# Attention and a two-layer product on one core: one more ff pair by seven half-size products, and another order and store for the last tile

## The chip, the cores and the metric

The kernel runs on one core of a Trainium2 chip. The metric is the device time of one execution in microseconds (us). TensorE (PE) multiplies matrices, VectorE (DVE), ScalarE (ACT) and GpSimd (POOL) work element by element, and SyncE (SP) issues most of the transfers (DMAs). In the profile, PEld is the loading of weights into TensorE, and a "q" behind an engine's name (SPq) is its instruction queue.

## The reference, cut to what matters

```python
def _attn_ref(q, k, v):                      # B, H, S, D = 4, 8, 768, 64
    k_sum = k.reshape(B, H, nb, block, D).max(axis=3)      # block = 32
    v_sum = v.reshape(B, H, nb, block, D).mean(axis=3)
    scores_l = scale * np.matmul(q, k.transpose(0, 1, 3, 2))   # kept within 16 of the diagonal
    scores_s = scale * np.einsum('bhsd,bhnd->bhsn', q, k_sum) + np.log(block)
    ...                                      # softmax over both, then times [v, v_sum]

def _moe_ref(x, w_in, w_out):                # x: 3072 x 512, w_in: 512 x 2048, w_out: 2048 x 512
    h = x @ w_in
    g = h * (1.0 / (1.0 + np.exp(-1.702 * h)))
    return (g @ w_out).astype(np.float32)
```

The attention's output, with the heads put side by side, is the `x` of the second function.

## The kernel before, in words

The work goes batch by batch (4 batches of S = 768 rows). For each batch the attention gives x, turned so that the model dimension lies on the partitions: four tiles `xTT[half][g]`, with the left half of the rows (384, called l) and the right half (r). The last two of them come by DMA transposes from SP. Then the two products follow: "ff", which is x times w_in and the gelu into `gTb`, and "out", which is g times w_out. While one batch is in its products, the attention of the next is put between them. The last batch has no next one, and its products stand alone; the change is there (from `mid.close()` to the end of the kernel function).

Every engine's instructions run in the order in which the code issues them (the class `_Ordered` holds them to it), so the order of the work is the order of the Python statements.

*ff in the last batch.* The 16 ff tiles of 128 columns of w_in are taken as 8 pairs (j and j + 8). A pair's result is four blocks of 128 x 384: two tiles by two halves. `plain(nt, half, tag)` works one block out directly: 4 matmuls of 384 columns and a gelu on ACT. The other way (`ff_product`, `ff_copy`, `ff_gelu`) is a fast 2 x 2 block product with seven products instead of eight: the model dimension is split in two as well, sums of weights (`wsi`) and sums of x (`xs`, by `x_sums` on DVE) are made beforehand, and each of the products 1 to 7 is 2 matmuls of 384 columns. They add up in four PSUM banks, called A, B, C and E; DVE makes a copy from A to C ("a") and the sums from A and "s" to B and E ("b" and "c"), ACT copies E to SBUF ("s"), and at the end four gelus read C, B, E and A. Product 7 adds to A after "b" has read it.

The table `steps` says in which slot of a pair each of these steps is issued, and pair after pair follows 7 slots later, so that the steps of three pairs interleave. `PLAIN` is the number of pairs that are worked out directly; before it is 2, so pairs 0 and 1 (eight blocks of 4 matmuls) are plain and 2 to 7 go by seven products. Seven of the eight plain blocks stand ahead of the first product, the eighth in slot 1 between products 1 and 5. The sums of x stand after the fourth plain block.

*out in the last batch.* The same scheme again: for each of three pairs of row tiles (t, of 128 rows on the left and on the right) `product` makes seven products of 8 matmuls of 256 columns. They read g or sums of g (`gs`, four kinds) and w_out or its sums (`ws`). The sums of g of the plain pairs are made on POOL, all four kinds; of the other pairs POOL makes kinds 0 and 1 (the last pair's are made on DVE), and two wide instructions on DVE make kinds 2 and 3 for all of them at once. Product 1 of each t comes early, between the last steps of ff. The others run in the order 5, 6, 2, 7, 3, 4. ACT copies the result of product 6 ("s2") from the bank to which product 7 then adds, and that of 5 ("s5"); DVE adds kept values to those of 2, 7 and 3 on the way into the output tiles (`give`), and ACT copies that of 4. The output tiles o1 (left rows) and o2 (right rows) are stored from SP (`store`), 128 x 512 floats at once; only in the last t is o2 stored in two halves.

Of the kernel before, what the change touches and what calls it, by code (L numbers as in the profile page):

```python
# [35 lines left out]
def kernel(  # L36
# [10 lines left out]
    B, H, S, D = q.shape  # L47
# [4 lines left out]
    d_model, d_ff = moe_w_in.shape  # L52
# [7 lines left out]
    HALF = S // 2  # L60
    TH = NQ // 2
    JH = NJ // 2
# [3 lines left out]
    act = _Ordered(tc, nc.scalar)  # L66
    pool = _Ordered(tc, nc.gpsimd)
    sp = _Ordered(tc, nc.sync)
# [200 lines left out]
    def copy(eng, out, in_):  # L269
        if eng is act:  # L270
            act.activation(out=out, in_=in_, func=ACT.Copy)
        elif eng == "dve_alone":

            dve.tensor_reduce(out=out, in_=in_.unsqueeze(len(in_.shape)), axis=AX.X, op=ALU.max)
        else:
            eng.tensor_copy(out=out, in_=in_)
# [366 lines left out]
    def gelu(half, nt, ph):  # L643
        act.activation(out=gT[half][:, nt, :], in_=ph, func=ACT.Gelu_apprx_sigmoid)
# [3 lines left out]
    def ff_step(ph, half, nt, steps=range(KO)):  # L648
        for n in steps:
            g, i = n // 2, n % 2  # L650
            ko = g + 2 * i if halves[0] else 2 * g + i
            pe.matmul(out=ph, lhsT=w_in_sb[:, ko, nt * 128:(nt + 1) * 128],
                      rhs=xTT[half][g][:, i], start=(n == 0), stop=(n == KO - 1))
# [29 lines left out]
    def g_sums(j, eng=dve, which=(0, 1, 2, 3)):  # L683

        a1, a2 = gTb[:, j], gTb[:, j + NT // 2]
        l, r = slice(0, HALF), slice(HALF, S)
        for w in which:
            a, b_, op = {0: (a1[:, r], a2[:, r], ALU.add), 1: (gs[:, 0, j], a1[:, l], ALU.subtract),
                         2: (a1[:, l], a1[:, r], ALU.subtract), 3: (a2[:, l], gs[:, 1, j], ALU.subtract)}[w]
            eng.tensor_tensor(out=gs[:, w, j], in0=a, in1=b_, op=op)  # L690
# [12 lines left out]
    now = {}  # L703
# [10 lines left out]
    xs = [vflat[:, i * 2 * HALF:(i + 1) * 2 * HALF].rearrange(two, k=2) for i in range(4)]  # L714
# [7 lines left out]
                     2: (a11, a21, ALU.subtract), 3: (a12, wsi[1], ALU.subtract)}[what]  # L722
        dve.tensor_tensor(out=wsi[what], in0=a, in1=b_, op=op)

    def x_sums():

        (l1, l2), (r1, r2) = xTT
        for o, a, b_ in ((0, r1, l1), (1, r2, xs[0]), (2, r2, r1), (3, l2, xs[1])):
            dve.tensor_tensor(out=xs[o], in0=a, in1=b_, op=ALU.subtract)

    plast = {}
# [1 line left out]
    def last_bank(tag, name):  # L733
        return plast[tag in "AB"].tile([128, 512], F32, name=name, tag="last" + tag,
                                       bufs={"A": 3, "E": 2, "B": 1, "C": 2}[tag])
# [39 lines left out]
    def product(b, t, what):  # L775
        n = NT // 2
        l = slice(t * 128, t * 128 + 128)
        r = slice(HALF + t * 128, HALF + t * 128 + 128)
        lo, hi = slice(0, N1), slice(N1, d_model)
        raw_l, raw_r = gTb[:, :, l], gTb[:, :, r]  # L780
        w1, w2 = w_out_sb[:, 0:n], w_out_sb[:, n:]
        lhs, rhs, bank, opens = {
            1: (raw_l[:, 0:n], w1[:, :, lo], "A", True),
            2: (raw_l[:, n:], w2[:, :, lo], "C", True),
            6: (gs[:, 1, :, l], ws[:, 1], "A", False),
            5: (gs[:, 0, :, l], ws[:, 0], "B", True),
            7: (gs[:, 2, :, l], ws[:, 2], "A", False),
            3: (gs[:, 3, :, l], w2[:, :, hi], "B", False),
            4: (raw_r[:, n:], ws[:, 3], "A", False)}[what]
        if opens:  # L790
            now[t, bank] = (last_bank("B" if bank == "A" and t == 2 else {"A": "A", "B": "E", "C": "C"}[bank],
                                      "po" + bank) if b + 1 == B
                            else pmm.tile([128, 512], F32, name="po" + bank, tag="mm"))
        po = now[t, bank][:, 0:N1]
        for i in range(n):
            pe.matmul(out=po, lhsT=lhs[:, i], rhs=rhs[:, i], start=(opens and i == 0),
                      stop=(i == n - 1), skip_group_check=True)

        def keep_it(name):
            if b + 1 == B and name == "s1":  # L800
                t_ = now[t, name] = spare[:, 2 * HALF + t * N1:2 * HALF + (t + 1) * N1]
            else:
                t_ = now[t, name] = snap.tile([128, N1], F32, name=name, tag=name)
            copy(dve if t == 0 and b + 1 < B else act, t_, po)

        def give(o, cols, name):
            if (t, o) not in now:
                now[t, o] = outp.tile([128, d_model], F32, name="osb", tag="osb")
            if name:
                dve.tensor_tensor(out=now[t, o][:, cols], in0=po, in1=now[t, name], op=ALU.add)  # L810
            else:
                act.activation(out=now[t, o][:, cols], in_=po, func=ACT.Copy)

        def store(o, tok, cols=slice(0, d_model)):
            r0 = b * S + tok
            sp.dma_start(out=out[r0:r0 + 128, cols], in_=now[t, o][:, cols])
            if cols.start == 0:
                now.pop((t, o))

        last = b == B - 1 and t == JH - 1  # L820

        if what == 1:
            keep_it("s1")
        elif what == 2:
            give("o1", lo, "s1")
        elif what == 6:
            keep_it("s2")
        elif what == 5:
            keep_it("s5")
        elif what == 7:  # L830
            give("o2", hi, "s5")
            if last:
                store("o2", HALF + t * 128, hi)
        elif what == 3:
            give("o1", hi, "s2")
            store("o1", t * 128)
        else:
            give("o2", lo, None)
            store("o2", HALF + t * 128, lo if last else slice(0, d_model))

    seq = [(0, 1)]
    for t in range(JH):
# [165 lines left out]
    for e in range(2):  # L1008
        r = slice(64 * e, 64 * e + 64)
        dve.tensor_copy(out=w50[r, JH - e:NJ, e, :, 0:D],  # L1010
                        in_=v0n[r, :, JH - e:NJ, 0:D].rearrange("p h j d -> p j h d"))
# [104 lines left out]
    for b in range(1, B - 1):  # L1116
# [32 lines left out]
        i = 0  # L1149
        for t, what in seq:  # L1150
            product(b, t, what)
            if i == 0:
                g_sums(NT // 2 - 1, dve, (2, 3))
            if nxt:
                beside(b + 1, i)
            i += 1
            if nxt and b + 2 < B:
                if i == 1:
                    load_batch(b + 2)
                if i in (16, 18):  # L1160
                    xk(i // 2 - 8, b % 2)
# [2 lines left out]
    for ab in (True, False):  # L1164
        plast[ab] = ctx.enter_context(tc.tile_pool(name=f"plast{ab:d}", bufs=2, space=bass.MemoryType.PSUM))
    b, n = B - 1, NT // 2
    PLAIN = 2

    def plain(nt, half, tag):
        ph = last_bank(tag, "ph")[:, 0:HALF]  # L1170
        ff_step(ph, half, nt)
        gelu(half, nt, ph)

    def ff_do(j, what):
        if isinstance(what, int):
            ff_product(j, what)
        elif what in "asbc":
            ff_copy(j, what)
        elif what == "g":
            g_sums(j, pool, (0, 1))  # L1180
        else:
            ff_gelu(j, what)

    for i, tag in enumerate("CCEEAAA"):
        plain((0, n, 1, n + 1)[i % 4], i // 4, tag)
        if i == 3:
            x_sums()
        if i in (5, 6):
            g_sums(0, pool, (0, 1) if i == 5 else (2, 3))
    steps = {0: [1, "a"], 1: [5, "s"], 9: [7, "c"], 10: [3], 4: [2], 5: [6, "b"], 13: [4],  # L1190
             6: ["C"], 11: ["B"], 12: ["E"], 14: ["A"], 15: ["g"]}
    for slot in range(7 * (n - PLAIN)):
        if slot == 1:
            plain(n + 1, 1, "B")
            g_sums(1, pool, (0, 1, 2, 3))
        for j in range(PLAIN, n):
            for what in steps.get(slot - 7 * (j - PLAIN), ()):
                ff_do(j, what)
    ff_do(n - 2, "A")
    product(b, 0, 1)  # L1200
    ff_do(n - 1, 7)
    ff_do(n - 1, "c")
    ff_do(n - 1, 3)
    ff_do(n - 2, "g")
    ff_do(n - 1, "B")
    ff_do(n - 1, "E")
    product(b, 1, 1)
    g_sums(n - 1, dve, (0, 1))
    ff_do(n - 1, 4)
    ff_do(n - 1, "A")  # L1210
    product(b, 2, 1)
    q_ = slice(PLAIN, n)
    dve.tensor_tensor(out=gs[:, 2, q_], in0=gTb[:, q_, 0:HALF], in1=gTb[:, q_, HALF:S], op=ALU.subtract)
    dve.tensor_tensor(out=gs[:, 3, q_], in0=gTb[:, PLAIN + n:2 * n, 0:HALF], in1=gs[:, 1, q_], op=ALU.subtract)
    for t, what in seq:
        if what != 1:
            product(b, t, what)


# [28 lines left out]
```

## Time and profile before

| | us |
|---|---|
| median of three runs | 206.14 |
| lowest and highest | 206.1, 207.8 |
| the profiled execution | 207.68 |
| its span, from the first to the last instruction | 205.9 |

| engine | busy, us | share of the span | instructions |
|---|---|---|---|
| PE | 199.3 | 97% | 2360 |
| DVE | 140.8 | 68% | 388 |
| ACT | 125.2 | 61% | 239 |
| POOL | 92.1 | 45% | 143 |

The first instruction of the last batch's ff starts at 164.76 us, the last matmul of the kernel ends at 202.35, and the span ends at 205.9.

How to read the lines that follow. In a timeline a row gives the start and the length in us, then the engine, the source line (here always L28, a helper that issues everything), the operation, the tile written, the tiles read, the shape, and how many instructions were put together (x28); a bracket gives the idle time before it and what ended it. Matmuls overlap one another, so in the timeline a group's length reaches 0.16 to 0.17 us into the next one. The chain of work is the sequence of instructions that ended last, followed back from the end; there each row is the time in which that work was what all else waited for. In the rows of DMA issues come the number of transfers, the size of one in KB and the time from issue to landing.

### The profile page before, as it was taken

How to read it: one execution, taken by the hardware profiler on the slowest of the kernel's cores; microseconds unless marked ns; L12 is line 12 of the kernel's file. 1: busy time of each engine (PE TensorE's matmuls, PEld its weight loads, DVE VectorE, ACT ScalarE, POOL GpSimd, SP SyncE). 2: the span in 40 equal slices, each digit the busy share in tenths (PEclk: the TensorE clock that was granted, in tenths of full speed). 3: DMA queues.
4: the chain of work that ended last, by engine and by line, in shares of the span. 5: the costliest groups of instructions: out<-in, count | busy, mean ns of one | idle time of the engine just before them, and what ended most of it. 6: DMA issues, size and time to landing. Idle time of an engine off the chain costs nothing.

```text
span 205.9 us, 5854 instructions
## 1 busy us (share of the span) xinstructions
PE 199.3 (97%) x2360; PEld 138.5 (67%) x2360; DVE 140.8 (68%) x388; ACT 125.2 (61%) x239; POOL 92.1 (45%) x143
## 2 busy tenths in 40 slices
PE   6999999999999999999999999999999999999992
PEld 6668564556754466656888875666888865678882
DVE  6495796594856693899667789896769536758221
ACT  4474975728886726677772446778670577984220
POOL 7974589457999690006970035000000009991000
PEclk9999999999999999999999999999999999999999
DMA  6999999999999999999996979999022640000222
GB/s 174 170 167 205 208 207 207 189 154 243 147 99 162 183 163 171 167 150 159 147 144 87 138 168 127 124 251 172 0 105 73 151 135 3 0 0 3 102 103 102
DMA packets 95850, 28.13 MB, mean 137 GB/s; under 512 B 83648, under 2 KB 92880, under 8 KB 95824
## 3 DMA queue, kind: packets, MB, share of 16 engines
q0 software_dynamic: 69648, 13.24, 80.5%
q1 hardware_dynamic: 26176, 14.52, 33.2%
q8 instruction: 18, 0.29, 0.6%
q14 instruction: 8, 0.07, 0.1%
HBM read 27.26 MB, written 6.29 MB: 163 GB/s over the span
## 4 chain that ended last, share of the span: by engine, by line
PE 89%; DMA 5%; DVE 3%; ACT 1%; issue 0%; SPq 0%; DVEq 0%
PE ph L28 33%; PE poA L28 16%; PE poB L28 8%; PE po L28 8%; PE ps_av L28 4%; PE poC L28 4%; PE phA L28 4%; PE ps_s L28 4%; DMA vw<-vs 3%; DMA gT<-in_k_dram 2%; PE ps_x L28 1%; PE ps_k L28 1%; PE ps_t L28 1%; PE phB L28 1%; PE phC L28 1%; PE ps_q L28 1%
## 5 line engine op out<-in xcount | busy, mean ns | idle before, releaser
L28 PE MATMUL ph<-xT,w_in_sb 128*128 128x384 f16 x416 | 70.2, 326 | 0.1
L28 PEld LDWEIGHTS <-w_in_sb 128*128 128x128 f16 x452 | 43.7, 98 | 27.8 <-issue 0.2
L28 ACT ACTIVATE gT<-ph 128x384 f16<-128x384 f32 x104 | 49.8, 491 | 18.6 <-PE ph L28 18.2
L28 PEld LDWEIGHTS <-gT 128*128 128x128 f16 x312 | 28.8, 98 | 11.0
L28 ACT ACTIVATE a_sb<-ps_s 128x768 bf16<-128x768 f32 (+1 forms) x32 | 25.0, 826 | 12.7 <-PE ps_s L28 12.7
L28 PEld LDWEIGHTS <-gs 128*128 128x128 f16 x288 | 27.7, 98 | 3.4
L28 POOL DMA_DIRECT2D vw<-in_v_dram x36 | 24.6, 705 | 9.4 <-DMA kb<-in_k_dram 4.7
L28 POOL TENSOR_TENSOR gs<-gT 128x384 f16<-128x384 f16 x9 | 8.2, 908 | 43.1 <-ACT gT L28 43.1
L28 PE MATMUL po<-w_out_sb,gT 128*128 128x512 f16 x96 | 23.6, 380 | 0.0
L28 DVE TENSOR_TENSOR a_sb<-a_sb,mk 128x768 bf16<-128x768 bf16 x28 | 14.9, 555 | 6.5 <-ACT a_sb L28 5.9
L28 PE MATMUL poA<-ws,gs 128*128 128x256 f16 x144 | 18.7, 273 | 0.0
L28 DVE TENSOR_TENSOR x<-ps_av,rc 128x384 f16<-128x384 f32 x32 | 17.8, 558 | 1.1
L28 DVE TENSOR_TENSOR gs<-gT 128x384 f16<-128x384 f16 (+1 forms) x34 | 13.3, 393 | 6.9 <-ACT gT L28 6.6
L28 POOL DMA_DIRECT2D qb<-in_q_dram x16 | 15.1, 970 | 3.2 <-DMA v0n<-in_v_dram 1.7
L28 PEld LDWEIGHTS <-kx 64*128 64x128 bf16 (+1 forms) x372 | 9.4, 95 | 6.8 <-issue 4.0
L28 POOL DMA_DIRECT2D kb<-in_k_dram x14 | 13.6, 985 | 0.3 <-issue 0.3
L28 DVE TENSOR_REDUCE ks<-kx 128x24 bf16<-128x768 bf16 x12 | 11.4, 948 | 3.3 <-ACT kx L28 3.0
L28 ACT ACT_TABLE_LOAD x10 | 12.8, 1283 | 1.0 <-PEq L1232 0.8
L28 ACT ACTIVATE osb<-poA 128x256 f32<-128x256 f32 x9 | 3.5, 384 | 15.8 <-PE poA L28 15.8
L28 ACT ACTIVATE s<-poA 128x256 f32<-128x256 f32 x11 | 4.2, 385 | 11.2 <-PE poA L28 11.2
L28 PEld LDWEIGHTS <-a_sb 128*64 128x64 bf16 (+2 forms) x400 | 7.9, 108 | 3.2 <-issue 1.7
L28 PE MATMUL poA<-w_out_sb,gT 128*128 128x256 f16 x72 | 9.4, 273 | 0.0
(117 smaller groups left out, 287.7 us busy)
## 6 DMA issues: line engine op xcount, KB each, us to landing
out_dram<-osb SPq DMA_DIRECT2D x23, 256.0 KB, 3.4
kb<-in_k_dram POOLq DMA_DIRECT2D x14, 192.0 KB, 6.3
qb<-in_q_dram POOLq DMA_DIRECT2D x12, 192.0 KB, 9.4
vw<-in_v_dram POOLq DMA_DIRECT2D x36, 64.0 KB, 5.2
w_out_sb<-in_moe_w_out_dram POOLq DMA_DIRECT2D x4, 512.0 KB, 12.6
w_in_sb<-in_moe_w_in_dram POOLq DMA_DIRECT2D x3, 512.0 KB, 12.5
vw<-vs SPq DMA_DIRECT2D x6, 198.0 KB, 6.7
gT<-in_k_dram SPq DMA_DIRECT2D x2, 384.0 KB, 3.5
```

The lines of the kernel that those rows point to most:

```text
L28: r = f(*a, **kw)
```

## The change

- `PLAIN` goes from 2 to 1: pair 1 too is worked out by seven products, and only pair 0 is plain. Three plain blocks instead of seven stand ahead of the first product, and one still stands in slot 1.
- The sums of x move: three of them stand after the third plain block, the fourth after the plain block of slot 1, which on DVE is behind the copy "a" of the first combined pair.
- POOL makes all four kinds of sums of g for pair 0 alone. The two wide sums on DVE cover seven pairs (2688 columns) instead of six (2304).
- In the last row tile (t = 2) the products run in the order 6, 5, 7, 2, 3, 4. The other two keep theirs.
- In the last row tile o1 too is stored in two halves, each as soon as it is there. The last store of the kernel (the left half of o2) is issued by ACT, which made its last copy, and no longer by SP. That copy is one instruction before and after.

```diff
-    def x_sums():
+    def x_sums(which):
...
-        for o, a, b_ in ((0, r1, l1), (1, r2, xs[0]), (2, r2, r1), (3, l2, xs[1])):
+        for o, a, b_ in [((0, r1, l1), (1, r2, xs[0]), (2, r2, r1), (3, l2, xs[1]))[w] for w in which]:
...
-        def store(o, tok, cols=slice(0, d_model)):
+        last = b == B - 1 and t == JH - 1
+
+        def store(o, tok, cols=slice(0, d_model), queue=sp):
             r0 = b * S + tok
-            sp.dma_start(out=out[r0:r0 + 128, cols], in_=now[t, o][:, cols])
-            if cols.start == 0:
+            queue.dma_start(out=out[r0:r0 + 128, cols], in_=now[t, o][:, cols])
+            if not last:
                 now.pop((t, o))
...
         elif what == 2:
             give("o1", lo, "s1")
+            if last:
+                store("o1", t * 128, lo)
...
         elif what == 3:
             give("o1", hi, "s2")
-            store("o1", t * 128)
+            store("o1", t * 128, hi if last else slice(0, d_model))
+        elif last:
+            give("o2", lo, None)
+            store("o2", HALF + t * 128, lo, act)
         else:
             give("o2", lo, None)
-            store("o2", HALF + t * 128, lo if last else slice(0, d_model))
+            store("o2", HALF + t * 128)
...
-    PLAIN = 2
+    PLAIN = 1
...
-    for i, tag in enumerate("CCEEAAA"):
-        plain((0, n, 1, n + 1)[i % 4], i // 4, tag)
-        if i == 3:
-            x_sums()
-        if i in (5, 6):
-            g_sums(0, pool, (0, 1) if i == 5 else (2, 3))
+    for i, tag in enumerate("CCE"):
+        plain(n * (i % 2), i // 2, tag)
+    x_sums(range(3))
...
         if slot == 1:
-            plain(n + 1, 1, "B")
-            g_sums(1, pool, (0, 1, 2, 3))
+            plain(n, 1, "B")
+            x_sums((3,))
+            g_sums(0, pool, (0, 1, 2, 3))
...
-    for t, what in seq:
-        if what != 1:
+    for t in range(JH):
+        for what in (5, 6, 2, 7, 3, 4) if t + 1 < JH else (6, 5, 7, 2, 3, 4):
             product(b, t, what)
```

More of the change, by code (lines that the diff above doesn't have):

```diff
@@ L812, in give @@
                 act.activation(out=now[t, o][:, cols], in_=po, func=ACT.Copy)
-        def store(o, tok, cols=slice(0, d_model)):
+        last = b == B - 1 and t == JH - 1
+        def store(o, tok, cols=slice(0, d_model), queue=sp):
             r0 = b * S + tok
-            sp.dma_start(out=out[r0:r0 + 128, cols], in_=now[t, o][:, cols])
-            if cols.start == 0:
+            queue.dma_start(out=out[r0:r0 + 128, cols], in_=now[t, o][:, cols])
+            if not last:
                 now.pop((t, o))
-        last = b == B - 1 and t == JH - 1
         if what == 1:
```

## The prediction

> **What bounds the kernel now.** I read the page's total and its chain of work first, then the chain row by row over the last batch, then the timelines of the engines around it, and the DMA issues last. The profiled execution took 207.68 us, of which the span is 205.9 and 1.78 lies around it; the median of the three runs shown is 206.14, so I work out a difference in the span and take it off the median.
>
> ```profile
> span 205.9 us, 5854 instructions
> ...
> PE 89%; DMA 5%; DVE 3%; ACT 1%; issue 0%; SPq 0%; DVEq 0%
> ```
>
> The chain that ends last is matmul after matmul for 89% of the span. In the stage that the change touches, the matmuls in order of time, and then the end of the chain:
>
> ```profile
> 164.76 4.71 PE L28 MATMUL ph<-xT,w_in_sb 128*128 128x384 f16 x28
> 169.31 0.49 PE L28 MATMUL phA<-xT,w_in_sb 128*128 128x384 f16 x2
> ...
> 171.59 0.49 PE L28 MATMUL phE<-vw,kx 128*128 128x384 f16 x2
> 172.14 0.48 PE L28 MATMUL phA<-vw,kx 128*128 128x384 f16 x2
> ```
> ```profile
> 171.52 0.58 DVE phB L28
> ...
> 201.47 0.89 PE poA L28 x8
> 202.35 0.02 issue
> 202.38 0.38 ACT osb L28
> ```
>
> The reader should see a stage that TensorE fills: 28 plain matmuls of 384 columns start between 164.76 and 169.31, 162.5 ns each, back to back. One place breaks the row: the product at 172.14 (7 of the first combined pair) starts 0.55 after the one before it, where two matmuls take 0.33, because it waited for the DVE sum of 171.52: a stall of 0.22. After the last matmul there is one copy (to 202.76), one store and the program's end.
>
> **The change, part by part.**
>
> *Matmuls.* A plain pair of ff tiles takes 2 tiles x 2 halves x 4 matmuls = 16; by seven products it takes 7 x 2 = 14. Pair 1 changes over, so two matmuls go: 2 x 162.5 ns = **-0.33 us**, all of it on the chain, if TensorE still sets the pace. It does in the rounds that exist:
>
> ```profile
> 175.26 0.49 ACT L28 ACTIVATE gT<-phB 128x384 f16<-128x384 f32 x1
> ...
> 182.09 0.49 ACT L28 ACTIVATE gT<-phB 128x384 f16<-128x384 f32 x1
> ```
>
> Three rounds lie between these two rows: 6.83 / 3 = 2.277 us a round, which is 14 x 162.5 ns = 2.275. ACT has five PSUM reads a round (four gelus and the copy "s") and follows without falling behind, so a seventh round adds 2.275 and removes 2.60. DVE gains three adds or copies, ACT one copy; both run beside TensorE at that pace, cost nothing there, and would each cost only what they lag behind 2.275 if that cover went.
>
> *The shorter lead-in.* Before the first product there were 28 plain matmuls, now 12 (pair 0, three of its four tile halves). So everything that prepares that product has 2.60 us less cover. These are the sums of x, and the DMA transposes that they and the third plain tile read:
>
> ```profile
> 164.86 0.56 DVE L28 TENSOR_TENSOR vw<-xT,xT 128x768 f16<-128x768 f16 x1 [0.27 <-DMA xT<-x]
> 166.27 0.56 DVE L28 TENSOR_TENSOR vw<-xT,vw 128x768 f16<-128x768 f16 x1 [0.86 <-DMA xT<-x]
> 166.75 0.55 DVE L28 TENSOR_TENSOR vw<-xT,xT 128x768 f16<-128x768 f16 x1
> 167.22 0.55 DVE L28 TENSOR_TENSOR vw<-xT,vw 128x768 f16<-128x768 f16 x1
> 169.91 0.57 DVE L28 COPY phC<-phA 128x384 f32<-128x384 f32 x1 [2.14 <-PE phA L28]
> ```
>
> The first plain matmul starts at 164.76; product 1 started at 169.31. The third plain tile now starts 8 matmuls in, at 166.06; its third matmul, at 166.39, is the first reader of the last transpose. That transpose had arrived when DVE started at 166.27: cover 0.12. Product 1 falls at 164.76 + 12 x 0.1625 = 166.71. The copy "a" began 0.60 after it (169.91 - 169.31), so now 167.31; DVE is free of the third sum at 167.22, where the fourth began: cover 0.09. The fourth sum is moved behind "a": it starts near 167.79, ends near 168.34, and its reader, product 4, stands 4 us further on. "a" ends at 167.88, product 2 starts at 168.01: the same 0.13 as before. With no wait longer than its cover I cost this part at 0; for each 0.1 us that the transpose is later than 0.12, TensorE loses 0.1. The stall of 0.22 stays, since the plain tile that was put between products 1 and 5 still is.
>
> *Sums for the second stage.* POOL had 18 sums and gets 16 (pairs 0 and 1 were done whole; now only 0), DVE's two wide sums grow from 2304 to 2688 columns:
>
> ```profile
> 185.49 0.68 DVE L28 TENSOR_TENSOR gs<-gT 128x384 f16<-128x384 f16 x1 [0.66 <-ACT gT L28]
> 186.20 0.36 DVE L28 TENSOR_TENSOR gs<-gs,gT 128x384 f16<-128x384 f16 x1
> 186.48 1.35 DVE L28 TENSOR_TENSOR gs<-gT 128x2304 f16<-128x2304 f16 x1
> 187.75 1.35 DVE L28 TENSOR_TENSOR gs<-gT,gs 128x2304 f16<-128x2304 f16 x1
> ```
> ```profile
> 185.04 0.91 POOL L28 TENSOR_TENSOR gs<-gs,gT 128x384 f16<-128x384 f16 x1
> ```
> ```profile
> 189.95 1.04 PE L28 MATMUL poB<-w_out_sb,gs 128*128 128x256 f16 x8
> ```
>
> 1.35 x 2688/2304 = 1.58, so +0.45 us for both. The second ended at 189.10 and ends at 189.10 - 0.33 + 0.45 = 189.22; its reader, product 3, comes at 189.95 - 0.33 = 189.62. Cover 0.40, hence 0; without the cover it would cost the overrun, 0.45 at most. POOL's last sum, which the second wide sum reads, ended at 185.95 and comes earlier.
>
> *The last tile.* Seven products in either order are 56 matmuls, so TensorE's end moves by the 0.33 alone. Product 7 now follows 5 directly behind 6, and adds to the bank that ACT is still copying ("s2"):
>
> ```profile
> 197.81 1.04 PE L28 MATMUL poA<-ws,gs 128*128 128x256 f16 x8
> 198.68 1.04 PE L28 MATMUL poC<-w_out_sb,gT 128*128 128x256 f16 x8
> ```
> ```profile
> 198.88 0.38 ACT L28 ACTIVATE s<-poA 128x256 f32<-128x256 f32 x1 [0.49 <-PE poA L28]
> ```
>
> A product takes 0.87. The copy begins 1.07 after product 6 and ends 1.45 after it; product 7 comes 2 x 0.87 = 1.74 after: cover 0.29, cost 0. The final copy stays one instruction of 0.38, as it was.
>
> *Stores.* Those of the last tile were 128, 256, 128 KB on SP; now three of 128 KB on SP and the last of 128 KB on ACT.
>
> ```profile
> out_dram<-osb SPq DMA_DIRECT2D x2, 128.0 KB, 1.7
> out_dram<-osb SPq DMA_DIRECT2D x1, 256.0 KB, 2.0
> ```
> ```profile
> 202.03 1.09 SPq L28 DMA_DIRECT2D out_dram<-osb  x2
> ```
> ```profile
> L28 SPq DMA_DIRECT2D out_dram<-osb x7: 332/332/333, 191.5 to 202.8; - x7
> ```
>
> The last store was issued about 0.03 after its copy (202.79 to 203.12) and SP was idle by 202.03 + 0.33 = 202.36, so SP held nothing up; it landed 1.7 later, as the first 128 KB store did that had no other behind or ahead of it. Splitting the 256 KB store therefore gains nothing. What is new is a store issued by ACT: no row of before has one. Ends: nothing, less the hand-over of 0.03; or the dearest queue in the trace, POOL's:
>
> ```profile
> L28 POOL DMA_DIRECT2D vw<-in_v_dram x36 | 24.6, 705 | 9.4 <-DMA kb<-in_k_dram 4.7
> ...
> vw<-in_v_dram POOLq DMA_DIRECT2D x36, 64.0 KB, 5.2
> ```
>
> POOL's issue takes 0.71 instead of 0.33 (+0.37), and those loads land after 5.2 instead of 1.7 (+3.5). I take SP's price, 0: its row is of the same transfer, 128 KB of the same tile out to memory with idle DMA engines, while POOL's rows are loads in a crowded stage. Of the end this leaves nothing to win: -0.03 at best, +3.9 at worst.
>
> The Trainium skill has a rule that speaks against expecting anything of this step (DMA: Bandwidth & Descriptors, "Issuing engines are not separate DMA queues"): transfers started by ACT, SP or GpSimd run on the same 16 DMA engines and interleave, so a second issuing engine saves only the time in which the first would have been busy issuing. By that rule the step is worth 0 as well, since SP was idle, and the sum stays where it is; no run here shows a store from ACT yet.
>
> **Sum.** -0.33 + 0 + 0 + 0 + 0: the span goes from 205.9 to 205.57, and the median from 206.14 to **205.8**. About 1% is what a measurement of this kernel can tell from no change; this is 0.16%.
>
> **The rivals.**
>
> *The last transpose comes too late for the shorter lead-in.* The cover is 0.12, and the landing times of these transposes differ:
>
> ```profile
> xT<-x SPq DMA_TRANSPOSE x2, 2.7
> ```
> ```profile
> xT<-x SPq DMA_TRANSPOSE x1, 4.1
> ```
>
> The first row is of the last two, the second of one that shared the engines with a store. For it speaks that nothing else fills these 2.6 us; against it that nothing ahead of 164.8 is changed, so that the transposes should land as they did. If the last took 4.1, it would be 1.4 later, 1.28 beyond the cover: 205.8 + 1.28 = 207.1. From 0.45 on (0.33 + 0.12) the two saved matmuls are given back, which is also the case in which the change does nothing: 206.1.
>
> *The store from ACT is dear* (the other side). It is the last thing on the path, so every bit of it counts whole. If only its issue is as slow as POOL's, 205.8 + 0.37 = 206.2; if it lands like POOL's loads, 205.8 + 3.9 = 209.7. The kernel is slower than before once this store takes 0.33 longer than SP's 1.7, and by over 1% once it takes 2.4 longer. For it: this would be ACT's only transfer, and nothing in the trace shows that queue at work. Against it: the equal work on SP has one price, 332 ns to issue in all seven rows.
>
> *The stall of 0.22 goes too.* Then 205.8 - 0.22 = 205.6. For it: DVE, ACT and POOL are all less loaded in the lead-in. Against it: product 7 waits for a sum that needs product 6, and between them stand only products 1 and 5 of the next pair, as before.
>
> *ACT becomes the bound of the rounds.* Five reads of 0.49 us each are 2.45 in 2.275, and they fit only because they overlap. Were the seventh round to lag by 0.1, the time would be 205.9; the three equal rounds above speak against it.
>
> **How the numbers follow.** I give the forecast 0.74, the late transpose 0.08, the dear store 0.09, the vanished stall 0.05, ACT as the bound 0.04. The likeliest is 205.8 us. The range reaches down to 205.4: the best sum is 206.14 - 0.33 - 0.22 - 0.03 = 205.56, and three runs fix a median no better than to a tenth or two. Upward it reaches to 207.1, the late transpose at its dearest row, which takes in the dear store up to 1.3 more than SP's; what is left out is that store at worse than that and runs like the slowest of the three shown (207.8). A gain of over 1% (below 204.1) has no case: 0.02 for what I overlooked. A loss of over 1% (above 208.2) needs the ACT store near its upper end: 0.05. Within 1%: 0.93.
>
> **What would show it.** In the changed kernel's trace: 12 plain matmuls ahead of the first phA product, starting near 164.8 and 166.7; no wait of the third plain tile for a transpose; one stall of about 0.2 in the first round, and the seven rounds 2.28 apart; the first matmul of the second stage 0.33 earlier; the second wide sum (128x2688, 1.58) done before product 3; ACT's copy of "s2" done before product 7 in the last tile; the last matmul's end near 202.0, the last copy's near 202.4; and the store from ACT issued in about 0.33 and landed in about 1.7. I would be wrong if TensorE's last matmul came at 202.3 or later (a wait took the place of the two matmuls), or if the time from the last copy to the span's end grew beyond the 3.14 of before (205.9 - 202.76).

## The result, and the profile after

| | before | changed |
|---|---|---|
| median of 22 runs each | 206.55 | 205.70 |
| lowest to highest | 205.96 to 208.08 | 205.06 to 207.98 |
| ratio | | 0.9958, 95% interval 0.9941 to 0.9976 |
| ratio on a second occasion (12 and 23 runs) | | 0.9971, 0.9945 to 0.9997 |
| profiled execution; its span | 207.68; 205.9 | 205.72; 203.7 |

The kernel is faster by 0.42% (0.87 us, interval 0.50 to 1.22), and by 0.29% (0.03% to 0.55%) the second time. It stays within 1%, as forecast, and the time lies next to the forecast's 205.8. That nearness is luck in part: the forecast started from the median of three runs, 206.14, which is 0.41 below that of 22, and its gain of 0.33 us is 0.54 short of the 0.87; the two errors nearly cancel. The first interval excludes a gain of 0.33, the second doesn't: the question is where the rest comes from. The change reaches no work ahead of the last batch, yet its first matmul comes 1.46 us earlier in this trace. That says nothing about the change: in the five traces of kernels that are equal up to there (before, e2_tail, e3_act, e5_split and e9_poolless in the table below) it started between 162.8 and 165.7. So the two traces are compared by stretches, not by clock time.

The page of the changed kernel, total and chain of work:

```profile
span 203.7 us, 5850 instructions
...
PE 82%; DMA 9%; DVE 5%; ACT 1%; issue 1%; SPq 0%; ACTq 0%; DVEq 0%
```

TensorE's timeline in the lead-in, and the chain's end:

```profile
163.30 2.11 PE L28 MATMUL ph<-xT,w_in_sb 128*128 128x384 f16 x12
165.25 0.49 PE L28 MATMUL phA<-xT,w_in_sb 128*128 128x384 f16 x2
165.58 0.81 PE L28 MATMUL ph<-xT,w_in_sb 128*128 128x384 f16 x4
...
167.53 0.49 PE L28 MATMUL phE<-vw,kx 128*128 128x384 f16 x2
168.08 0.48 PE L28 MATMUL phA<-vw,kx 128*128 128x384 f16 x2
```
```profile
199.68 0.89 PE poA L28 x8
200.57 0.02 issue
200.59 0.38 ACT osb L28
```

From the first plain matmul to the end of the last matmul it takes 200.57 - 163.30 = 37.27 us by these rows, against 202.35 - 164.76 = 37.59 before; by the trace's nanoseconds 37.251 and 37.576, a difference of 0.325: the two matmuls, to the nanosecond. The lead-in has no new wait, and the old one is there with the old size (167.53 to 168.08 is 0.55 again).

The moved sums and the sums for the second stage, on DVE, with their readers on TensorE and the copy "s2" on ACT:

```profile
164.56 0.56 DVE L28 TENSOR_TENSOR vw<-xT,vw 128x768 f16<-128x768 f16 x1 [0.82 <-DMA xT<-x]
165.04 0.55 DVE L28 TENSOR_TENSOR vw<-xT,xT 128x768 f16<-128x768 f16 x1
165.84 0.57 DVE L28 COPY phC<-phA 128x384 f32<-128x384 f32 x1 [0.26 <-PE phA L28]
...
183.70 0.36 DVE L28 TENSOR_TENSOR gs<-gT 128x384 f16<-128x384 f16 x1 [0.66 <-ACT gT L28]
...
185.84 1.55 DVE L28 TENSOR_TENSOR gs<-gT,gs 128x2688 f16<-128x2688 f16 x1
```
```profile
188.16 1.04 PE L28 MATMUL poB<-w_out_sb,gs 128*128 128x256 f16 x8
...
196.90 1.04 PE L28 MATMUL poA<-ws,gs 128*128 128x256 f16 x8
```
```profile
196.22 0.38 ACT L28 ACTIVATE s<-poA 128x256 f32<-128x256 f32 x1 [0.49 <-PE poA L28]
```

Every cover held. The second wide sum ends at 187.39, 0.77 ahead of product 3 (0.40 forecast: the first small sum takes 0.36 instead of 0.68; before, POOL's last sum ran beside it, and here that had ended at 183.15). "s2" is ready at 196.60, 0.30 ahead of product 7 (0.29 forecast).

Of the end, the last store and its neighbours in the DMA issues, and POOL's part of the instructions with which the program stops, under the names that the trace gives them (semaphores, drains, the clear of a range of semaphores; the same query of before below it):

```profile
out_dram<-osb SPq DMA_DIRECT2D x3, 128.0 KB, 1.7
out_dram<-osb ACTq DMA_DIRECT2D x1, 128.0 KB, 1.7
```
```profile
201.00 0.37 ACTq L28 DMA_DIRECT2D out_dram<-osb  x1
```
```profile
L1247 POOLq EVENT_SEMAPHORE  x4: 17/17/17, 202.9 to 203.6; - x4
...
L1247 POOLq DRAIN  x2: 51/76/102, 203.1 to 203.4; - x2
...
L1247 POOLq EVENT_SEMAPHORE_RANGE_CLEAR  x1: 139/139/139, 203.2 to 203.2; - x1
```
```profile
L1243 POOLq EVENT_SEMAPHORE  x4: 17/17/17, 204.8 to 205.8; - x4
...
L1243 POOLq DRAIN  x2: 102/150/198, 204.9 to 205.5; - x2
...
L1243 POOLq EVENT_SEMAPHORE_RANGE_CLEAR  x1: 139/139/139, 205.1 to 205.1; - x1
```

The reader should look at POOL's last instructions: after the semaphore clear it reaches its last drain in 0.17 us and takes 51 ns for it, where before it took 0.46 and 198 ns. From the clear to the span's end it is 0.45 instead of 0.89, so 0.44 us of the shorter span lies in a place where the kernel computes nothing. With it the time from the last copy's end to the span's end falls from 3.18 to 2.71.

### The profile page after: what moved, and what is told of

The parts are those of the page before. It is cut to its first block, busy times and chain, and to the rows that moved or that the text cites. A ratio compares the mean times of both kernels' runs of the same rounds, so it can differ in the third digit from the quotient of the medians.

```text
span 203.7 us, 5850 instructions
## 1 busy us (share of the span) xinstructions
PE 196.8 (97%) x2358; PEld 136.7 (67%) x2358; DVE 141.6 (70%) x391; ACT 125.4 (62%) x240; POOL 90.3 (44%) x141
## 4 chain that ended last, share of the span: by engine, by line
PE 82%; DMA 9%; DVE 5%; ACT 1%; issue 1%; SPq 0%; ACTq 0%; DVEq 0%
PE ph L28 23%; PE poA L28 16%; PE po L28 11%; PE poB L28 8%; PE ps_av L28 4%; PE phA L28 4%; DMA out_dram<-osb 4%; PE poC L28 4%; PE ps_s L28 3%; DMA qT<-qb 3%; DMA gT<-in_k_dram 2%; DVE ks L28 2%; PE ps_t L28 1%; PE ps_x L28 1%; DVE qT L28 1%; DVE gs L28 1%
## 5 line engine op out<-in xcount | busy, mean ns | idle before, releaser
L28 PE MATMUL ph<-xT,w_in_sb 128*128 128x384 f16 x400 | 67.6, 326 | 0.1
L28 PEld LDWEIGHTS <-w_in_sb 128*128 128x128 f16 x442 | 42.7, 98 | 27.1 <-issue 0.2
L28 ACT ACTIVATE gT<-ph 128x384 f16<-128x384 f32 x100 | 47.9, 492 | 17.9 <-PE ph L28 17.1
L28 POOL TENSOR_TENSOR gs<-gT 128x384 f16<-128x384 f16 x8 | 7.3, 911 | 43.1 <-PE phC L28 42.0
L28 PEld LDWEIGHTS <-kx 64*128 64x128 bf16 (+1 forms) x378 | 10.0, 95 | 7.8 <-issue 4.9
```

The source lines that it names most:

```text
L28: r = f(*a, **kw)
```

## The experiments

Theory 1 was the prediction's: the two matmuls are all, the rest is scatter. Theory 2: the last tile's stores give the rest. Theories 3 and 4 came with the traces of the first four kernels. All kernels in one table; the stretches are from each kernel's one profiled execution, "beyond" is the mean of device time less span over all its runs. POOL's instructions are counted in the traces; the expectations count one more for each kernel.

| kernel | POOL's instructions | first ff matmul to last matmul's end | last copy's end to SP's first drain | clear to span's end | beyond the span | ratio to before (95%) |
|---|---|---|---|---|---|---|
| before | 199 | 37.58 | 1.90 | 0.89 | 1.71 | |
| changed | 195 | 37.25 | 1.86 | 0.45 | 2.01 | 0.9958 (0.9941 to 0.9976) |
| e1_pairs | 195 | 37.25 | 1.90 | 0.45 | 1.99 | 0.9976 (0.9951 to 1.0002) |
| e2_tail | 199 | 37.58 | 1.86 | 0.90 | 1.71 | 1.0000 (0.9971 to 1.0028) |
| e3_act | 199 | 37.58 | 1.94 | 0.89 | 1.72 | 1.0004 (0.9972 to 1.0037) |
| e6_sp | 195 | 37.25 | 1.81 | 0.45 | 2.01 | 0.9973 (0.9940 to 1.0006) |
| e5_split | 199 | 37.58 | 1.81 | 0.89 | 1.68 | one run |
| e9_poolless | 196 | 37.58 | 1.89 | 0.45 | 2.14 | 0.9993 (0.9966 to 1.0021) |
| e10_pad4 | 199 | 37.25 | 1.86 | 0.89 | 1.71 | 0.9998 (0.9972 to 1.0024) |
| e11_pad8 | 203 | 37.25 | 1.86 | 0.45 | 1.74 | one run |
| e11_pad16 | 211 | 37.25 | 1.86 | 0.45 | 1.71 | one run |
| e12_best | 195 | 37.12 | 1.81 | 0.45 | 2.01 | 0.9975 (0.9955 to 0.9995) |
| e14_plain0 | 192 | 37.82; 38.45 from where TensorE was free | 1.86 | 0.45 | 1.88 | 1.0024 (1.0002 to 1.0046) |

### The pairs without the last tile, and the reverse

e1_pairs is the changed kernel with `seq` and the old stores for the last tile; e2_tail is before with the new order and stores.

> The seventh pair alone (PLAIN = 1 with the moved sums), with the last tile's order and stores as before. Theory 1 (the two saved matmuls are the whole gain, the last tile gives nothing): 0.33 us less than before, ratio 0.9984; in the trace the first plain matmul to the start of the last product takes 36.22 instead of 36.54, and the last copy's end to the span's end stays at 3.1 to 3.2. Theory 2 (the last tile's stores give the rest of the 0.9 us that were measured): the same 0.33 here, and the other 0.5 missing.

> The last tile's part alone (order, o1 stored in halves, last store from ACT), six pairs by seven products as before. Theory 1: no change, ratio 1.000 within 0.1%; the end from the last copy to the span's end is 3.1 give or take the scatter of such ends. Theory 2: 0.4 to 0.5 us less than before, ratio 0.998, with 2.7 us from the last copy's end to the span's end, as in the changed kernel.

The matmuls did in both what either theory says (37.25 and 37.58). Theory 2 falls: the short end of 0.45 goes with the pairs (e1_pairs), not with the last tile (e2_tail), which by itself gives 0.04 in the trace and nothing that can be measured. The ratios alone don't decide between the two theories, since e2_tail's interval holds 1.000 and 0.998 alike. Theory 1 did not expect the short end either.

### The stores

```diff
-            store("o2", HALF + t * 128, lo if last else slice(0, d_model))
+            store("o2", HALF + t * 128, lo if last else slice(0, d_model), act if last else sp)   # e3_act
...
-            store("o2", HALF + t * 128, lo, act)
+            store("o2", HALF + t * 128, lo)                                                       # e6_sp
...
+            if last:                                                                              # e5_split
+                store("o1", t * 128, lo)
...
-            store("o1", t * 128)
+            store("o1", t * 128, hi if last else slice(0, d_model))
```

> Before, with the last store issued by ACT and nothing else. Theory 1: no change (ratio 1.000), store issued in about 0.37 and landed in about 1.7 as in the changed kernel; the time from copy to landing differs from SP's by less than 0.1. Theory 2, if it is the issuing engine that shortens the end: 0.4 less, ratio 0.998, and 2.7 us from copy to the span's end.

> The changed kernel with its last store back on SP. Theory 1: same as the changed kernel, 0.33 less than before, ratio 0.9984. Theory 2, if the issuing engine matters: 0.4 us slower than the changed kernel, so at best ratio 0.9984 against 0.996, with 3.1 us from copy to the span's end instead of 2.7.

> Before, with o1 of the last tile stored in two halves, nothing else. The prediction: the halves gain nothing, so the last copy's end to SP's first drain stays at 1.90 (from ACT with the whole o1 it was 1.94, from ACT with halves and the new order 1.86, from SP with halves and the new order 1.81). If the halves are what gains: 1.81 to 1.85. If the new order of products is: 1.90.

From the last copy's end to SP's first drain, which SP reaches when all stores have landed: 1.90 with SP and the whole o1, 1.94 with ACT and the whole o1, 1.81 with SP and the halves in either order, 1.86 with ACT and the halves. So ACT costs 0.04 to 0.05 (issued in 0.37 instead of 0.33), the halves gain 0.09, and the new order of products nothing. Of the 0.09, 0.06 is one wait fewer that SP has to go through behind the last landing. e6_sp's ratio (interval up to 1.0006) can't tell any of this; only the stretches can.

### POOL's stream

Theory 3: it is the length of POOL's stream of instructions that decides how its last ones come through; theory 4: it is the work on POOL or its timing.

```diff
-            g_sums(1, pool, (0, 1, 2, 3))                    # e9_poolless, from before
+            g_sums(1, pool, (0, 1))
...
-    q_ = slice(PLAIN, n)
+    q_ = slice(1, n)
...
     mid.close()                                              # e10_pad4, e11_pad8, e11_pad16, from changed
+    pad = consts.tile([128, 1], F32, name="pad")
+    for i in range(4):                                       # 8, 16
+        pool.memset(pad, 0.0)
```

> Before (six pairs, old last tile), with the two last kinds of sums of pair 1 taken off POOL and put into DVE's two wide sums: POOL's stream has 197 instructions instead of 200, TensorE's work is untouched. Theory 3 (the rest of the gain is POOL's stream: with the 196 of the changed kernel its instructions behind the last semaphore clear come through 0.44 sooner, whatever the work was): stretch from the clear to the span's end near 0.45 instead of 0.89, if three fewer are enough, and the median 0.4 lower, ratio 0.998; first plain matmul to last matmul's end stays 37.58. Theory 1 (scatter): the stretch falls to either value without order, ratio 1.000.

> The changed kernel with four tiny memsets (one float on each partition) on POOL, put where POOL idles before the last batch, so that its stream has 200 instructions again. Theory 3: the stretch from the semaphore clear to the span's end goes back to 0.89, and the ratio to before from 0.996 to 0.998; the rest of the trace is as in the changed kernel (37.25 from the first plain matmul to the last matmul's end). Theory 4 (it is not the number of POOL's instructions but that its last sum is done earlier, or that it makes fewer sums): the stretch stays 0.45.

> The changed kernel with eight tiny memsets on POOL while it idles, 204 instructions in its stream. Theory 3 (the place of the stream's end counts): the stretch from the semaphore clear to the span's end is a stretch of 0.45 or 0.89, not something between, and the segment on TensorE stays 37.25. I expect 0.45, as the slow end would lie in the block boundary's neighbourhood alone, with a device time about 1.7 to 2.1 beyond the span.

> The same with sixteen memsets, 212 instructions. If the count only matters near one place (200 instructions), the stretch from the clear to the end is 0.45; if every longer stream is slow, 0.89.

The end of e10_pad4, as above:

```profile
L1250 POOLq DRAIN  x2: 102/150/198, 204.3 to 204.9; - x2
L1250 POOLq EVENT_SEMAPHORE_RANGE_CLEAR  x1: 139/139/139, 204.5 to 204.5; - x1
```

Four idle memsets, 79 us ahead of the end (they run from 125.94 on), bring the 198 ns drain and the 0.89 back, with all sums as in the changed kernel: theory 4 falls, theory 3 stands. The ratios of e9_poolless and e10_pad4 can't tell: each interval holds 0.998 and 1.000 alike. And I had priced it by the span alone. The span ends when the last instruction of the program does, and the device time goes on. It goes on for 1.71 where the end is slow and 2.01 where it is fast (e9_poolless: 2.14), so of the 0.44 only 0.44 - 0.30 = 0.14 is gained in the time that counts, and e9_poolless, which was expected at 0.998, gains 0.44 - 0.43 = 0.01 and measured 0.9993. In the two longer streams both are short: 0.45 and 1.74 or 1.71, which is 0.27 and 0.30 better than the changed kernel, by one run each.

What goes with it is a place in POOL's stream. In all five kernels with 199 instructions the pause lies behind the 196th, the semaphore clear: the last drain starts 0.32 to 0.35 after the clear has ended, in all others 0.03 after it. An instruction fetch goes with the same place. From the span's start on queue 14 fetches 8 KB nine times in each of these traces, eight times at much the same moments (within 7 us). The ninth moves with POOL's count: it comes 1.80 us after the span's end with 192 instructions, 1.41 to 1.43 with 195, 0.99 with 196 and 0.27 to 0.46 with 199, but at 186.10 in e11_pad8 and at 177.73 in e11_pad16, behind the start of POOL's 196th and 197th instruction. The DMA queues of before and of the changed kernel, from just ahead of the span's end on, and those of e11_pad8 from 185 to 187 (one packet of 0.01 MB each):

```profile
q14 instruction: 1, 0.01, 0.8%
```
```profile
q14 instruction: 1, 0.01, 0.9%
```
```profile
q14 instruction: 1, 0.01, 1.7%
```

That POOL's stream crosses the edge of a fetched block there fits all of this. With 199 instructions the crossing falls among POOL's last ones and inside the span, with 192 to 196 behind the span, and with 203 and 211 ahead of POOL's last instructions, where neither part of the end grows. The trace names no engine for a fetch, so the mechanism is inferred from these places, and the dependence on the count is shown. The Trainium skill (Runtime: NRT & Kernel Launch, "Instruction fetch mechanics") has streams fetched in blocks, with the crossing of a block's edge mostly hidden. Inside the kernel these traces agree: with the moved fetch at 186.10 or 177.73 TensorE's stretch is 37.25 as in the changed kernel. At the program's end the crossing cost up to 0.44 here (0.89 + 1.71 against 0.45 + 1.71).

### The lead-in

e12_best is the changed kernel with the last store on SP and, in the first combined pair, 5 and "s" ahead of the plain block, 6 and "b" ahead of 2. e14_plain0 has no plain block at all; one sum of x stands ahead of the first product and three in slot 1, on DVE behind the copy "a".

```diff
         if slot == 1:                                        # e12_best
+            ff_do(PLAIN, 5)
+            ff_do(PLAIN, "s")
             plain(n, 1, "B")
...
+            at = slot - 7 * (j - PLAIN)
+            if j == PLAIN and at in (1, 4, 5):
+                todo1 = {1: (), 4: (6, "b"), 5: (2,)}[at]
...
-    PLAIN = 1                                                # e14_plain0
+    PLAIN = 0
...
-    x_sums(range(3))
+    x_sums((0,))
...
-            plain(n, 1, "B")
-            x_sums((3,))
-            g_sums(0, pool, (0, 1, 2, 3))
+            x_sums((1, 2, 3))
```

> The changed kernel with its last store on SP, and in the first combined pair product 5 and the copy s ahead of the plain block, product 6 and the sum b ahead of product 2, so that the sum is ready when product 7 wants it. Reason of the prediction for the stall of 0.22: product 7 waits for b, b for 6 and s. Then the stall falls to 0.07 or less, the segment from the first plain matmul to the last matmul's end from 37.25 to 37.05-37.10, the store's landing comes 0.05 earlier than from ACT; in all 0.2 less than the changed kernel, ratio to before 0.995. If the stall has another cause, the segment stays 37.25.

> The changed kernel once more, beside before on another occasion. The terms found so far in the traces (two matmuls 0.33, the stores 0.04, POOL's stream 0.44 inside the span of which 0.30 comes back behind it) sum to 0.5 less than before, ratio 0.9976. If they are all there is, the ratio is 0.997 to 0.998; if a further 0.4 is real, 0.996 again.

> The changed kernel with pair 0 by seven products too (PLAIN = 0): no plain block, so nothing covers the last transpose, which lands 1.3 to 1.5 after the first matmul. Two more matmuls go (-0.33 on TensorE). The first rival of the prediction, that the lead-in covers this transpose: product 6 waits for the sum behind it, until 1.9 to 2.1 after the start instead of 1.0, and product 7 for b behind that, so the segment from the first matmul to the last matmul's end is 37.25 - 0.33 + 1.0 to 1.5 = 37.9 to 38.4, slower than the changed kernel by 0.7 to 1.2. If the transpose and the sums do not matter, the segment is 36.93.

e12_best, TensorE and the sum "b" on DVE:

```profile
169.12 0.49 PE L28 MATMUL phE<-vw,kx 128*128 128x384 f16 x2
169.53 0.48 PE L28 MATMUL phA<-vw,kx 128*128 128x384 f16 x2
```
```profile
168.91 0.57 DVE L28 TENSOR_TENSOR phB<-phA,vw 128x384 f32<-128x384 f32 x1 [0.45 <-ACT gT L28]
```

The stall falls from 0.22 to 0.41 - 0.325 = 0.09, and the stretch by 0.13, so its cause was the place of 5, "s", 6 and "b" ahead of 7. Which of them alone would do isn't shown, since e12_best moves all. In the changed kernel "s" is what released "b":

```profile
167.46 0.57 DVE L28 TENSOR_TENSOR phB<-phA,vw 128x384 f32<-128x384 f32 x1 [0.59 <-ACT vw L28]
```

Product 6, which started at 166.88, would have let it start no earlier: in the next round "b" follows it by 0.58 too (169.05 to 169.63). What is left in e12_best is the plain block's gelu, which holds the bank that "b" writes. The stretch of 37.12 misses the 37.05 to 37.10 expected by little, the ratio of 0.9975 (0.9955 to 0.9995) misses 0.995 clearly, which had been counted from the changed kernel's first ratio. By its stretches e12_best takes 0.69 less than before, and 0.52 was measured: it beats before clearly, and the changed kernel in the trace alone.

after_again is the changed kernel, unchanged (a blank line at its end): 0.9971. It lies between the two values that were set against each other, 0.9976 and 0.996, and its interval holds both.

e14_plain0's output is not the reference's, though all products, sums and copies are issued; why is not known, so it is read for its waits alone:

```profile
164.53 0.48 PE L28 MATMUL phA<-xT,w_in_sb 128*128 128x384 f16 x2 [0.47 <-ACT osb L28]
164.85 0.49 PE L28 MATMUL phE<-vw,kx 128*128 128x384 f16 x2
165.72 0.48 PE L28 MATMUL phC<-xT,w_in_sb 128*128 128x384 f16 x2 [0.39 <-DVE phC L28]
166.18 0.48 PE L28 MATMUL phA<-vw,kx 128*128 128x384 f16 x2
...
166.83 0.49 PE L28 MATMUL phE<-vw,kx 128*128 128x384 f16 x2
167.59 0.48 PE L28 MATMUL phA<-vw,kx 128*128 128x384 f16 x2 [0.28 <-DVE phB L28]
```

Counted from 163.89, where TensorE was free, its stretch is 38.45, 1.20 above the changed kernel; from its own first matmul it is 37.82, just under the 37.9 to 38.4 expected. The reason is not the expected one. Against the 0.33 of the two matmuls stand 0.64 at the first matmul, whose bank ACT is still emptying for the batch before, 0.55 for the copy "a", 0.13 for a sum of x that stands behind "a" on DVE and that product 6 reads, and 0.44 at product 7, where the changed kernel has 0.22. After 163.87 no instruction waits for a transpose, so what a late transpose costs is not shown by this kernel.

## Why the prediction was right, and what it missed

- *Matmuls, -0.33:* right. 37.58 and 37.25 in every kernel with six and seven pairs, whatever else was changed, but for e12_best, where the order of the lead-in is another.
- *The shorter lead-in, 0:* right. The third plain tile did not wait (the transpose was there 1.26 after the first matmul, its reader came at 1.62), and the stall stayed. The late transpose, the first rival, did not happen in any of these traces, but its cover is no constant: in the traces with seven pairs the sum behind the last transpose starts 1.05 to 1.66 after the first matmul. At 1.66 (e11_pad16) nothing of the cover is left, and TensorE's row does not break yet.
- *Sums for the second stage, 0:* this is the term that was mis-sized. The two sums off POOL were costed by their readers alone, and those were covered, as forecast. But the same step shortens POOL's stream from 199 to 195 instructions, and the program's end follows that: -0.44 in the span, and by the means of device time less span -0.14 in the time.
- *The last tile, 0:* right; the new order changes neither TensorE's stretch (37.58 in e2_tail) nor the end (1.81 in e5_split without it and in e6_sp with it).
- *Stores, 0:* halves -0.09, ACT +0.05, together -0.04. The dear ACT store, the rival on the other side, did not come: 0.05 where it needed 0.33.
- *The sum:* -0.33 - 0.14 - 0.04 = -0.51 explained, against -0.87 (-1.22 to -0.50) and -0.60 (0.9971 of 206.53; -1.14 to -0.06) measured. -0.51 lies at the edge of the first interval and well inside the second. e1_pairs and e6_sp fit such sums (-0.47 and -0.56 explained, -0.50 and -0.56 by their ratios), e10_pad4 less well (-0.37 and -0.04), all three with intervals of 0.5% to 0.7%. What lies between -0.51 and the first median is not tied to any stretch of the traces; the second measurement doesn't need it. With runs that scatter by 2 to 3 us in the stages ahead of the change, that rest stays open.
- *The stand-in of span for time:* the prediction took 1.78 around the span as fixed. It is 1.68 to 2.14 by kernel, and the runs of a kernel lie within 0.1 of their mean, but for e14_plain0 (1.65 to 2.01).

## What to carry to other kernels

In a stretch that TensorE fills, count its matmuls: that term was exact. A cover that hangs on the engines' own rows held (0.29 forecast and 0.30 found for "s2"); one with a sum beside POOL's work came out at 0.77 instead of 0.40, and one that hangs on a transfer moved by 0.6 us from trace to trace. Where the whole scatters by more than the effect, compare the stretches that the change touches, in several kernels' traces, and not the medians alone. Check what lies behind the span as well as the span: here 0.30 of a gain of 0.44 came back where no row of the page shows it.

## What was not expected of the hardware

- The end of the program depends on the number of POOL's instructions: 0.89 + 1.71 us from the semaphore clear to the end of the device time with 199, 0.45 + 2.14 with 196, 0.45 + 2.01 with 195, 0.45 + 1.88 with 192, 0.45 + 1.74 and 0.45 + 1.71 with 203 and 211 (one run each). Eight memsets that do nothing would by this take another 0.27 off the changed kernel; one run of that kernel can't show it.
- A store issued by ACT takes 0.37 to issue where SP takes 0.33, and lands in the same 1.7.
- The start of the last batch, after identical work, lies anywhere between 162.8 and 165.7 in these traces.
